# TensorE in written order with whole score units and projections three steps behind, and the second batch's first scores in the softmax gap

## The chip, the cores and the metric

One core of one Trainium2 chip runs the kernel. The metric is the device time in microseconds (us) of one execution, as a median of several. A difference under about 0.2% (4.6 us here) can't be told from no change.

## What is computed

There are four batches. In each, the columns of q and k (6080 tokens by 256 channels) are scaled to length one, a 256 by 256 matrix of scores between channels is formed over all tokens, a softmax is taken over its rows, and v is multiplied by it. The result, 24320 tokens by 256, goes through a two-layer network with a gated unit of 2048 columns.

```python
qn = q / (np.linalg.norm(q, axis=1, keepdims=True) + 1e-06)
kn = k / (np.linalg.norm(k, axis=1, keepdims=True) + 1e-06)
s = kn.transpose(0, 2, 1) @ qn / tau
a = np.exp(s - s.max(-1, keepdims=True))
a /= a.sum(-1, keepdims=True) + 1e-09
x = (v @ a).reshape(B * S, D)
h = x @ w_in
g = h * (1.0 / (1.0 + np.exp(-1.702 * h)))
out = g @ w_out
```

## The kernel before, in words

The attention of a batch ends in a 256 by 256 matrix, so the kernel folds it into the first layer: `weights` (L366) multiplies that matrix by w_in, and v goes straight through the product. Nearly all matrix work is done on numbers split in two parts, "hi" and "lo" (`split`, L77: ScalarE rounds to the hi part in a cast, VectorE subtracts to get the lo part), with three products hi·hi, hi·lo and lo·hi.

**The main loop** runs over four batches, 12 chunks of 512 tokens (the last has 448) and 16 slices `f` of 128 hidden columns: 768 steps. A step calls `hidden` (L396: six matmuls of 512 columns into a `ps_h` bank; then ScalarE's sigmoid L413, VectorE's product L414, ScalarE's cast to `gh` and VectorE's subtraction to `gl`) and, two steps behind (`DEPTH = 2`), `project` (L422: six matmuls into two `ps_o` banks that add up over the 16 slices). There are three `ps_h` banks, three `ps_o` banks and two banks `s0`, `s1` for the scores. In the first 32 steps the first two chunks take turns, so that each slice of w_in is used twice.

**The lead-in** (a `manual_schedule` block, so all engines in the written order) does the attention of batch 0 alone: `load` brings 128-partition pieces of q and k, `prepare` squares them (ScalarE) and adds the squares up (VectorE for batch 0), and `score` multiplies them as plain float32 (`direct`, L245: two records of 256 columns for each matmul, two output halves for each of the 48 token rows). Then come the norms (`norms_a`, L269: matmuls with a column of ones, `ps_n`; GpSimd takes a root; `norms_b` makes a diagonal matrix; `norms_c` spreads it by a matmul, `ps_b`), `softmax_a` and `softmax_c` on VectorE and ScalarE, four transposes (`ps_t`) and the first `weights` (`ps_w`, L372). While the softmax runs, `keep_warm` (L447) gives TensorE 18 and then 4 matmuls of ones.

**Side work of the main loop**: a dictionary from the step to functions that run after that step's `project`. In batch 0 it has the conversion of w_in and w_out from 64-bit words (`to_float32`, L102 to L132, steps 0 to 26), `win_split` and `weights` for the next three groups of slices; in batches 0 to 2 also the next batch's attention: `prepare` of a unit (two token rows of 128) and, three steps later, its `score`. There each row and half has one matmul of 512 columns (L250, hi part of k against hi and lo of q) and one of 256 (L258, lo part of k). Its squares are added up on GpSimd (L229). Batch 1's first unit is prepared at step 34. The order on each engine in the loop isn't the written one: a scheduler picks it from the dependencies and its own estimates when the program is built, and after that it is fixed.

Of the kernel before, what the change touches and what calls it, by code (L numbers as in the profile page):

```python
# [27 lines left out]
def channel_attention_then_glu(  # L28
# [137 lines left out]
    class Attention:  # L166
        def __init__(self, b, direct=False):
            self.b = b

            self.direct = direct  # L170
            self.raw = {}

            self.loads = [(0, UT)] + [(t, RT) for t in range(UT, T + 1, RT)]
            self.wh = [None] * NG
            self.wl = [None] * NG

            self.units = [(t, min(UT, T - t), P) for t in range(0, T, UT)]
            if TAIL:
                self.units.append((T, 1, TAIL))

        def load(self, t0, room):
# [4 lines left out]
            cuts = range(nt + 1) if self.direct and t0 == 0 else (0, nt)  # L186
            tiles = {}
            for a, z in zip(cuts, cuts[1:]):
                for src, tag in ((q, "raw_q"), (k, "raw_k")):
                    if tag not in tiles:  # L190
                        if self.direct:
# [14 lines left out]
        def prepare(self, u):  # L206
# [3 lines left out]
            rq, rk = (t[:pp, :nt, :] for t in self.raw[t0])  # L210
            if self.direct:
# [7 lines left out]
            for r, nm in ((rq, "acc_q"), (rk, "acc_k")):  # L219
# [4 lines left out]
                else:  # L224
# [3 lines left out]
                    eng = nc.vector if self.direct else nc.gpsimd  # L228
                    eng.tensor_tensor(acc, acc, sq, op=ALU.add)  # L229
            return qs, ks  # L230

        def score(self, u, qs, ks):
            t0, nt, pp = self.units[u]
            if u == 0:
# [4 lines left out]
            for j in range(nt):  # L239
                first = u == 0 and j == 0  # L240
                last = u == len(self.units) - 1 and j == nt - 1
                for i in range(NC2):
                    ci = slice(i * P, (i + 1) * P)
                    if self.direct:
                        nc.tensor.matmul(  # L245
                            self.s[i][:, :C], lhsT=ks[:, j, ci], rhs=qs[:, j, :],
                            start=first, stop=last,
                        )
                        continue
                    nc.tensor.matmul(  # L250
                        self.s[i],
                        lhsT=ks[:pp, j, 0, ci],
                        rhs=qs[:pp, j, :, :],
                        start=first,
                        stop=False,
                        skip_group_check=True,
                    )
                    nc.tensor.matmul(  # L258
                        self.s[i][:, C:],
                        lhsT=ks[:pp, j, 1, ci],  # L260
                        rhs=qs[:pp, j, 0, :],
                        start=False,
                        stop=last,
                        skip_group_check=True,
                    )

        def norms_a(self):
# [3 lines left out]
            for n in range(2 * NC2):  # L271
                acc, i = (self.acc_q, self.acc_k)[n // NC2], n % NC2
                if i == 0:
                    eng = nc.vector if self.direct else nc.gpsimd
# [31 lines left out]
        def softmax_a(self):  # L306
            self.x = small.tile([P, NC2, C], F32, tag="x", name="x")
            self.z = small.tile([P, NC2], F32, tag="z", name="z")
            m = small.tile([P, NC2], F32, tag="m", name="m")
            for i in range(NC2):  # L310
                x, z, mi = self.x[:, i, :], self.z[:, i : i + 1], m[:, i : i + 1]
                s = self.s[i][:, :C]
                if not self.direct:
                    nc.scalar.copy(x, self.s[i][:, C:])
# [74 lines left out]
    def v_split(b, c):  # L389
        w = chunks[c][1]  # L390
        raw = vtiles[b, c]
        vh = vp.tile([P, NC2, NCH], F32R, tag="v_h", name="v_h")
        vl = vp.tile([P, NC2, NCH], F32R, tag="v_l", name="v_l")
        split(vh[:, :, :w], vl[:, :, :w], raw[:, :, :w])
        vtiles[b, c] = (vh, vl)

    def hidden(at, b, c, f):
        w = chunks[c][1]
        vh, vl = vtiles[b, c]
# [15 lines left out]
        gh = gp.tile([P, NCH], F32R, tag="gh", name="gh")  # L415
        gl = gp.tile([P, NCH], F32R, tag="gl", name="gl")
# [37 lines left out]
    at = Attention(0, direct=True)  # L454
    nu = len(at.units)
# [4 lines left out]
    with tc.manual_schedule():  # L460
# [18 lines left out]
        win_fetch(3)  # L479
        wout_fetch(1)  # L480
        for u in range(nu - AHEAD, nu - 3):
# [149 lines left out]
```

## Time and profile before

| what | value |
|---|---|
| median of 3 runs (lowest, highest) | 2298.05 us (2297.94, 2298.36) |
| the profiled execution's own time | 2298.09 us |
| its span from first to last instruction | 2296.3 us |
| TensorE (PE), busy share of the span | 100% |
| VectorE (DVE), ScalarE (ACT), GpSimd (POOL) | 60%, 53%, 9% |
| granted TensorE clock | 1.0 |
| DMA queues, share of 16 engines' span | 14.0% |

The profile is of one execution. A row of a group gives line, engine, operation, output<-inputs, shape and count, then the busy time, the mean of one in ns, and the idle time before with what ended it. A timeline row gives start, duration, engine, line and how many instructions are merged; in brackets is the idle time before it with what released it. Matmuls overlap, so that the time one costs is the distance to the next start, not its duration. A matmul in plain float32 has two records, one in split form has one.

### The profile page before, as it was taken

The page shows a single profiled execution, that of the slowest core. Times are in us where ns is not written, and L with a number is a line of the kernel's source. Part 1 is how long each engine was busy: PE and PEld are TensorE (multiplying, and loading weights), DVE is VectorE, ACT ScalarE, POOL GpSimd, SP SyncE. Part 2 cuts the span into 40 slices and gives each one's busy share as a digit, 9 for nine tenths or more (in the row PEclk, how much of TensorE's full clock was granted, in tenths as well). Part 3 has the DMA queues.
Part 4 walks back from the last instruction along what each step waited for, and adds up shares of the span by engine and source line. Part 5 has one row for each costly group of instructions (what it writes and reads, how often), then busy time and mean ns, then how long its engine had stood idle before and what let it go on. Part 6 is the DMA issues. An engine that isn't in the chain of part 4 may idle for free.

```text
span 2296.3 us, 27390 instructions
## 1 busy us (share of the span) xinstructions
PE 2286.2 (100%) x10300; PEld 1906.7 (83%) x10300; DVE 1374.9 (60%) x2033; ACT 1224.0 (53%) x2108; POOL 212.3 (9%) x160
## 2 busy tenths in 40 slices
PE   9999999999999999999999999999999999999999
PEld 8878888888888888888888888888888888888888
DVE  7986666565565556565556556656555555555554
ACT  6765555555555555555455555554544444444444
POOL 0022322010020022010002012100000000000000
PEclk9999999999999999999999999999999999999999
DMA  8222111100111121110011111110000000000000
GB/s 309 92 74 74 56 55 61 57 27 19 37 54 56 37 74 56 35 56 18 19 56 46 46 56 56 55 35 28 18 19 28 27 19 28 28 19 28 27 9 18
DMA packets 46389, 109.77 MB, mean 48 GB/s; under 512 B 4528, under 2 KB 8624, under 8 KB 46256
## 3 DMA queue, kind: packets, MB, share of 16 engines
q1 hardware_dynamic: 46256, 108.02, 14.0%
q8 instruction: 80, 1.31, 0.2%
q14 instruction: 53, 0.43, 0.1%
HBM read 83.10 MB, written 24.90 MB: 47 GB/s over the span
## 4 chain that ended last, share of the span: by engine, by line
PE 96%; issue 2%; DVE 1%; ACT 0%; POOL 0%; POOLq 0%; DVEq 0%; ACTq 0%
PE ps_o L432 45%; PE ps_h L407 45%; PE s L250 3%; PE ps_w L372 2%; PE s L258 2%; DVE gl L79 0%; PE ps_x L451 0%; DVE z L127 0%; DVE g L414 0%; PE ps_n L276 0%; PE ps_b L299 0%; POOL rn L284 0%; DVE wl L79 0%; PE ps_t L344 0%; DVE z L121 0%
## 5 line engine op out<-in xcount | busy, mean ns | idle before, releaser
L414 DVE TENSOR_TENSOR g<-ps_h,g 128x512 f32<-128x512 f32 (+1 forms) x768 | 524.0, 683 | 456.9 <-ACT g L413 453.6
L79 DVE TENSOR_TENSOR gl<-g,gh 128x512 fp32r<-128x512 f32 (+1 forms) x768 | 566.1, 739 | 383.2 <-ACT gh L78 379.1
L413 ACT ACTIVATE g<-ps_h 128x512 f32<-128x512 f32 (+1 forms) x768 | 453.6, 592 | 508.4 <-PE ps_h L407 504.4
L78 ACT CAST gh<-g 128x512 fp32r<-128x512 f32 (+1 forms) x768 | 472.0, 615 | 442.7 <-DVE g L414 326.7
L407 PE MATMUL ps_h<-v_h,wh 128*128 128x512 f32 (+1 forms) x1536 | 598.0, 389 | 0.3 <-DVE g L414 0.3
L407 PE MATMUL ps_h<-v_h,wl 128*128 128x512 f32 (+1 forms) x1536 | 596.0, 388 | 1.6 <-DVE wl L79 1.6
L432 PE MATMUL ps_o<-gl,wo_h 128*128 128x512 f32 (+1 forms) x1536 | 596.0, 388 | 1.2 <-DVE gl L79 1.2
L407 PE MATMUL ps_h<-v_l,wh 128*128 128x512 f32 (+1 forms) x1536 | 596.3, 388 | 0.0
L432 PE MATMUL ps_o<-gh,wo_l 128*128 128x512 f32 (+1 forms) x1536 | 595.8, 388 | 0.0
L432 PE MATMUL ps_o<-gh,wo_h 128*128 128x512 f32 (+1 forms) x1536 | 504.2, 389 | 0.0
L407 PEld LDWEIGHTS ps_h<-v_h,wl 128*128 128x128 f32 x1536 | 288.6, 188 | 60.2 <-DVE wl L79 2.5
L407 PEld LDWEIGHTS ps_h<-v_h,wh 128*128 128x128 f32 x1536 | 288.7, 188 | 59.0 <-DVE g L414 1.3
L432 PEld LDWEIGHTS ps_o<-gl,wo_h 128*128 128x128 f32 x1536 | 288.6, 188 | 59.0 <-DVE gl L79 2.4
L432 PEld LDWEIGHTS ps_o<-gh,wo_l 128*128 128x128 f32 x1536 | 288.6, 188 | 57.1
L407 PEld LDWEIGHTS ps_h<-v_l,wh 128*128 128x128 f32 x1536 | 288.7, 188 | 54.2
L432 PEld LDWEIGHTS ps_o<-gh,wo_h 128*128 128x128 f32 x1536 | 286.6, 188 | 56.2 <-ACT win_h L78 0.2
L229 POOL TENSOR_TENSOR acc_q<-acc_q,sq 128x512 f32<-128x512 f32 (+1 forms) x72 | 93.8, 1303 | 1235.2 <-ACT sq L227 1082.8
L229 POOL TENSOR_TENSOR acc_k<-acc_k,sq 128x512 f32<-128x512 f32 (+1 forms) x72 | 112.2, 1558 | 11.1 <-ACT sq L227 10.8
L250 PE MATMUL s<-qs,ks 128*128 128x512 f32 (+1 forms) x288 | 109.1, 395 | 0.0
L258 PE MATMUL s<-qs,ks 128*128 128x256 f32 (+1 forms) x288 | 81.0, 281 | 0.0
L227 ACT ACTIVATE sq<-raw_q 128x512 f32<-128x512 f32 (+1 forms) x96 | 58.2, 606 | 34.0 <-DMA raw_q<-in_q 31.4
L79 DVE TENSOR_TENSOR v_l<-v_raw,v_h 128x1024 fp32r<-128x1024 f32 (+1 forms) x48 | 59.4, 1237 | 11.1 <-ACT v_h L78 10.0
(82 smaller groups left out, 928.0 us busy)
## 6 DMA issues: line engine op xcount, KB each, us to landing
raw_q<-in_q SPq DMA_DIRECT2D x44, 512.0 KB, 4.0
raw_k<-in_k SPq DMA_DIRECT2D x44, 512.0 KB, 4.4
v_raw<-in_vT SPq DMA_DIRECT2D x44, 512.0 KB, 3.8
out_T<-osb SPq DMA_DIRECT2D x88, 256.0 KB, 2.1
words<-in_w_in SPq DMA_DIRECT2D x8, 512.0 KB, 7.5
words<-in_w_out SPq DMA_DIRECT2D x8, 512.0 KB, 3.5
v_raw<-in_vT SPq DMA_DIRECT2D x4, 448.0 KB, 3.6
out_T<-osb SPq DMA_DIRECT2D x8, 224.0 KB, 2.0
```

The costliest lines, as they stand in the source:

```text
L78: ins = nc.scalar.copy(dst_hi, src)
L79: nc.vector.tensor_tensor(dst_lo, src, dst_hi.bitcast(F32), op=ALU.subtract)
L227: nc.scalar.activation(sq, r, AF.Square)
L229: eng.tensor_tensor(acc, acc, sq, op=ALU.add)
L250: nc.tensor.matmul(self.s[i], lhsT=ks[:pp, j, 0, ci], rhs=qs[:pp, j, :, :], start=first, stop=False, skip_group_check=True,)
L258: nc.tensor.matmul(self.s[i][:, C:], lhsT=ks[:pp, j, 1, ci], rhs=qs[:pp, j, 0, :], start=False, stop=last, skip_group_check=True,)
L372: nc.tensor.matmul(ps, lhsT=l[:, j, ci], rhs=r[:, j, :], start=n == 0, stop=n == 3 * NC2 - 1,)
L407: nc.tensor.matmul(ps[:, :w], lhsT=l[:, j, fs], rhs=r[:, j, :w], start=n == 0, stop=n == 3 * NC2 - 1,)
L413: newest[0] = nc.scalar.activation(g, ps[:, :w], AF.Sigmoid, scale=1.702)
L414: nc.vector.tensor_tensor(g, ps[:, :w], g, op=ALU.mult)
L432: nc.tensor.matmul(out[d][:, :w], lhsT=l[:, f, ds], rhs=r[:, :w], start=f == 0 and n == 0, stop=f == NF - 1 and n == 2,)
```

## The change

- TensorE runs the whole loop in the written order (`manual_schedule(engines={PE})`); the other engines are still scheduled. From step 26 (`WIDE`) on, `project` runs three steps behind instead of two, and `gh` and `gl` get two more buffers each in a pool that the conversions no longer use.
- `score` of a split unit issues all its 512-column matmuls and then all its 256-column ones.
- The first four units of batch 1 (`nxt = Attention(1, 4)`) are scored in plain float32 in the lead-in (`score_first`, 16 matmuls in groups of 3, 11, 1 and 1) in place of the 22 matmuls of `keep_warm`; their four loads are issued in the lead-in and stay in buffers of the `wh` and `wl` tags. Their squares are taken at steps 26, 28, 30 and 32, each behind the newest sigmoid on ScalarE (`pinned`). The other 21 units follow from step 35, also pinned in batch 0.
- In the lead-in, batch 0's unit nu-3 is scored ahead of the norms, and units nu-2 and nu-1 ahead of `norms_c`. The second load of batch 0 comes in two halves.
- Splits of v are cut in two halves, and later loads are issued four steps before their `prepare`.

```diff
-            self.loads = [(0, UT)] + [(t, RT) for t in range(UT, T + 1, RT)]
+            short = UT if self.alone else 0
+            self.loads = [(t, RT) for t in range(short, T + 1, RT)]
+            if short:
+                self.loads.insert(0, (0, short))
...
-            cuts = range(nt + 1) if self.direct and t0 == 0 else (0, nt)
+            cuts = (0, nt)
+            if self.alone and t0 <= UT:
+                cuts = range(0, nt + 1, 1 + t0 // UT)
...
+        def score_first(self, n):
+            ps = ps_o.tile([P, NCH], F32, tag="o", name="s_first")
+            todo = [(u, j, i) for u in range(self.direct) for j in range(UT) for i in range(NC2)]
+            for m, (u, j, i) in enumerate(todo):
+                rq, rk = self.fetched(u)
+                nc.tensor.matmul(
+                    ps[:, i * C : (i + 1) * C],
+                    lhsT=rk[:, j, i * P : (i + 1) * P],
+                    rhs=rq[:, j, :],
+                    start=m == 0, stop=m == len(todo) - 1,
+                    skip_group_check=True,
+                )
+                if m + 1 in n:
+                    yield
+            yield
+            self.x = small.tile([P, NC2, C], F32, tag="x", name="x")
+            nc.scalar.copy(self.x, ps.rearrange("p (c x) -> p c x", c=NC2))
...
+            for j, i in steps:
+                nc.tensor.matmul(
+                    self.s[i],
+                    lhsT=ks[:pp, j, 0, i * P : (i + 1) * P],
+                    rhs=qs[:pp, j, :, :],
...
+            for j, i in steps:
+                nc.tensor.matmul(
+                    self.s[i][:, C:],
+                    lhsT=ks[:pp, j, 1, i * P : (i + 1) * P],
+                    rhs=qs[:pp, j, 0, :],
...
-        for u in range(nu - AHEAD, nu - 3):
+        for u in range(0, nxt.direct, RT // UT):
+            nxt.fetched(u)
+        wout_fetch(1)
+        for u in range(nu - AHEAD, nu - 2):
             at.score(u, *ready[u])
         at.norms_a()
...
-        for u in range(nu - 3, nu - 1):
+        for u in range(nu - 2, nu):
             at.score(u, *ready[u])
+        s1 = nxt.score_first((3, 14, 15))
+        next(s1)
         at.norms_c()
-        at.score(nu - 1, *ready[nu - 1])
-        keep_warm(ones, 18)
+        next(s1)
         at.softmax_a()
         at.softmax_c()
         at.transposes(lambda: next(o0))
-        keep_warm(ones, 4)
+        next(s1)
...
+    with tc.manual_schedule(engines={mybir.EngineType.PE}):
...
+                for u in range(nu):
+                    if u < nd:
+                        put(WIDE + 2 * u, pinned, prep, u)
+                        continue
+                    at_u = first + 4 * (u - nd)
+                    put(at_u - 4, nxt.fetched, u)
+                    put(at_u, *((pinned, prep) if b == 0 else (prep,)), u)
+                    put(at_u + 3, score, u)
...
-                if len(late) > DEPTH:
+                if len(late) > (3 if wide[0] else 2):
                     project(*late.pop(0))
```

The order of instructions changes as follows. TensorE's order in the softmax gap, before: `s` are batch 0's scores, `ps_x` the matmuls of `keep_warm`, `ps_b` those of `norms_c`, `ps_t` the transposes, `ps_w` the weights.

```order
L276 MATMUL ps_n<-ones,acc_k 128x1 x2
L245 MATMUL s_167<-raw_q,raw_k 128x256
L245 MATMUL s_168<-raw_q,raw_k 128x256
L245 MATMUL s_167<-raw_q,raw_k 128x256
L245 MATMUL s_168<-raw_q,raw_k 128x256
L245 MATMUL s_167<-raw_q,raw_k 128x256
L245 MATMUL s_168<-raw_q,raw_k 128x256
L299 MATMUL ps_b<-diag,ones 128x128 x2
L245 MATMUL s_167<-raw_q,raw_k 128x256
L245 MATMUL s_168<-raw_q,raw_k 128x256
L451 MATMUL ps_x<-ones 128x128 x18
L344 MATMUL ps_t<-ident,x 128x128 x4
```

The same place after the change, where `s_first` are batch 1's first scores:

```order
L312 MATMUL ps_n<-ones,acc_k 128x1 x2
L275 MATMUL s_169<-raw_q,raw_k 128x256
L275 MATMUL s_170<-raw_q,raw_k 128x256
L275 MATMUL s_169<-raw_q,raw_k 128x256
L275 MATMUL s_170<-raw_q,raw_k 128x256
L250 MATMUL s_first<-raw_q,raw_k 128x256 x3
L335 MATMUL ps_b<-diag,ones 128x128 x2
L250 MATMUL s_first<-raw_q,raw_k 128x256 x11
L385 MATMUL ps_t<-ident,x 128x128 x4
L250 MATMUL s_first<-raw_q,raw_k 128x256
```

Between `ps_n` and `ps_b` stand four scores of batch 0 in place of six, none are left behind `ps_b`, and four more therefore stand ahead of `ps_n`; `s_first` fills the places of `ps_x`.

TensorE's order at one score unit of batch 1 before, with the numbers of the buffers (`gh_1510` is the `gh` of one step, whose `project` is cut in two here):

```order
L250 MATMUL s0_1560<-qs_1490,ks_1491 128x512
...
L432 MATMUL ps_o_1479<-gh_1510,wo_h_100 128x512
L258 MATMUL s0_1560<-qs_1490,ks_1491 128x256
...
L250 MATMUL s1_1561<-qs_1490,ks_1491 128x512
L258 MATMUL s1_1561<-qs_1490,ks_1491 128x256
L250 MATMUL s0_1560<-qs_1490,ks_1491 128x512
L258 MATMUL s0_1560<-qs_1490,ks_1491 128x256
L250 MATMUL s1_1561<-qs_1490,ks_1491 128x512
L258 MATMUL s1_1561<-qs_1490,ks_1491 128x256
```

A unit after the change:

```order
L285 MATMUL s0_1607<-qs_1535,ks_1536 128x512
L285 MATMUL s1_1608<-qs_1535,ks_1536 128x512
L285 MATMUL s0_1607<-qs_1535,ks_1536 128x512
L285 MATMUL s1_1608<-qs_1535,ks_1536 128x512
L294 MATMUL s0_1607<-qs_1535,ks_1536 128x256
L294 MATMUL s1_1608<-qs_1535,ks_1536 128x256
L294 MATMUL s0_1607<-qs_1535,ks_1536 128x256
L294 MATMUL s1_1608<-qs_1535,ks_1536 128x256
```

The eight matmuls of a unit stand together, with three pairs of neighbours of 256 columns, where the two widths took turns before, with projections of three steps between the first two.

ScalarE's order before, at the end of the conversions (`sq` are the squares that GpSimd adds up, `z` on L118 begins a conversion, here the last two):

```order
L227 ACTIVATE sq_1603<-raw_k_1592 128x512
L227 ACTIVATE sq_1704<-raw_q_1590 128x512
L227 ACTIVATE sq_1707<-raw_k_1592 128x512
...
L118 ACTIVATE z_1142<-words_1067 128x512
...
L227 ACTIVATE sq_1808<-raw_q_1798 128x512
L413 ACTIVATE g_1191<-ps_h_1184 128x512
L118 ACTIVATE z_1207<-words_1117 128x512
```

After the change, from the last conversion to the second unit's squares (`acc` is written by the first unit's squares alone, without an addition):

```order
L118 ACTIVATE z_1214<-words_1124 128x512
...
L462 ACTIVATE g_1300<-ps_h_1293 128x512
L234 ACTIVATE acc_q_1307<-raw_q_431 128x512
L234 ACTIVATE acc_k_1309<-raw_k_433 128x512
...
L462 ACTIVATE g_1338<-ps_h_1331 128x512
L238 ACTIVATE sq_1355<-raw_q_431 128x512
L238 ACTIVATE sq_1358<-raw_k_433 128x512
```

The squares of batch 1, and with them GpSimd's additions, stood among the conversions and stand behind the last of them now.

More of the change, by code (lines that the diff above doesn't have):

```diff
@@ L238, in score @@
                 ]
[L239 to L256, printed above, removed]
-                    )
[L258 to L265, printed above, removed]
+            steps = [(j, i) for j in range(nt) for i in range(NC2)]
@@ new lines, in score @@
+            last = u == len(self.units) - 1
+            if u < self.direct:
+                for j, i in steps:
+                    nc.tensor.matmul(
+                        self.s[i][:, :C],
+                        lhsT=ks[:, j, i * P : (i + 1) * P],
+                        rhs=qs[:, j, :],
+                        start=u == start and j == 0,
+                        stop=last and j == nt - 1,
+                    )
+                return
+            for j, i in steps:
[3 more added lines that the diff above has]
+                    rhs=qs[:pp, j, :, :],
+                    start=u == start and j == 0,
+                    stop=False,
+                    skip_group_check=True,
+                )
@@ L267, in norms_a @@
+            for j, i in steps:
+                nc.tensor.matmul(
+                    self.s[i][:, C:],
+                    lhsT=ks[:pp, j, 1, i * P : (i + 1) * P],
+                    rhs=qs[:pp, j, 0, :],
+                    start=False,
+                    stop=last and j == nt - 1,
+                    skip_group_check=True,
+                )
         def norms_a(self):
@@ L306, in softmax_a @@
         def softmax_a(self):
-            self.x = small.tile([P, NC2, C], F32, tag="x", name="x")
+            begun = not self.alone and self.direct
+            if not begun:
+                self.x = small.tile([P, NC2, C], F32, tag="x", name="x")
             self.z = small.tile([P, NC2], F32, tag="z", name="z")
@@ L387, in v_load, with v_split @@
         vtiles[b, c] = raw
-    def v_split(b, c):
+    vsplit = {}
+    def v_split(b, c, j=None):
         w = chunks[c][1]
         raw = vtiles[b, c]
[L392 to L395, printed above, removed]
+        if not j:
+            vh = vp.tile([P, NC2, NCH], F32R, tag="v_h", name="v_h")
+            vl = vp.tile([P, NC2, NCH], F32R, tag="v_l", name="v_l")
+            vsplit[b, c] = (vh, vl)
+        vh, vl = vsplit[b, c]
+        js = slice(None) if j is None else slice(j, j + 1)
+        split(vh[:, js, :w], vl[:, js, :w], raw[:, js, :w])
+    wide = [0]
     def hidden(at, b, c, f):
         w = chunks[c][1]
-        vh, vl = vtiles[b, c]
+        vh, vl = vsplit[b, c]
         grp, o = divmod(f, FG)
```

153 lines of the change are left out of this document (87 added, 66 removed).

## The prediction

> **What bounds the kernel now.** I read the page first: the busy times, then the chain that ended last.
>
> ```profile
> span 2296.3 us, 27390 instructions
> PE 2286.2 (100%) x10300; PEld 1906.7 (83%) x10300; DVE 1374.9 (60%) x2033; ACT 1224.0 (53%) x2108; POOL 212.3 (9%) x160
> PE 96%; issue 2%; DVE 1%; ACT 0%; POOL 0%; POOLq 0%; DVEq 0%; ACTq 0%
> ```
>
> TensorE is busy throughout and carries 96% of the chain. So a change helps only if it takes matmuls off TensorE or closes a gap in it. How full is it really? The chain gives the distance between matmuls in a quiet stretch, and the timeline of PE that of a score unit:
>
> ```profile
> 1884.57 2.27 PE ps_o L432 x10
> ```
>
> ```profile
> 174.14 0.39 PE L250 MATMUL s<-qs,ks 128*128 128x512 f32 x1
> 174.37 0.28 PE L258 MATMUL s<-qs,ks 128*128 128x256 f32 x1
> 174.48 0.39 PE L250 MATMUL s<-qs,ks 128*128 128x512 f32 x1
> 174.71 0.28 PE L258 MATMUL s<-qs,ks 128*128 128x256 f32 x1
> ```
>
> A 512-column matmul costs 0.227 us, a 256-column one 0.11 (174.37 to 174.48; I use half of 0.227, 0.113). The windows show where TensorE isn't full:
>
> ```profile
> 60.00:122.00 62.00, 61.45 (x269) 50.16 (x268) 57.00 (x100) 48.04 (x86) 4.90 (x2) 1.00 0.30 95
> 122.00:138.00 16.00, 13.37 (x57) 10.22 (x56) 16.00 (x20) 9.88 (x19) 9.94 (x7) 1.00 0.23 85
> 138.00:200.00 62.00, 62.00 (x278) 50.82 (x277) 38.63 (x57) 34.52 (x58) 5.96 (x4) 1.00 0.16 52
> ```
>
> Columns: width, then busy time and count of PE, PEld, DVE, ACT, POOL. In 122 to 138 us, 57 matmuls at 0.227 fill 12.9 of 16 us, and DVE is busy for all 16 with only 20 instructions. Later there is nothing to close. The rest to win is in the lead-in, in that stretch, and in the number of matmuls.
>
> **Scores taken out of the loop.** Four units, two rows, two halves: 16 matmuls of each width leave batch 1's loop, 16 x (0.227 + 0.113) = 5.4 us. Their place is full of TensorE work on both sides, so all of it counts: -5.4. ScalarE's casts and VectorE's subtractions of those units go too; both engines have slack (62% DVE in the third window).
>
> **The gap that takes them.** TensorE in the lead-in:
>
> ```profile
> 9.20 36.50 PE L245 MATMUL s<-raw_q,raw_k 128*128 128x256 f32 x168 [1.68 <-DMA raw_k<-in_k]
> 45.63 0.61 PE L276 MATMUL ps_n<-ones,acc_q 128*128 128x1 f32 x4
> ...
> 49.69 0.71 PE L299 MATMUL ps_b<-diag,ones 128*128 128x128 f32 x4 [0.31 <-DVE diag L292]
> 50.33 1.13 PE L245 MATMUL s<-raw_q,raw_k 64*128 64x256 f32 x4
> 51.38 4.29 PE L451 MATMUL ps_x<-ones 128*128 128x128 f32 x36
> 55.51 0.60 PE L344 MATMUL ps_t<-ident,x 128*128 128x128 f32 x4
> ...
> 56.78 0.73 PE L372 MATMUL ps_w<-win_h,aT_h 128*128 128x512 f32 x2
> ...
> 60.57 0.50 PE L407 MATMUL ps_h<-v_h,wl 128*128 128x512 f32 x1 [0.25 <-DVE wl L79]
> ...
> 64.79 0.51 PE L407 MATMUL ps_h<-v_h,wh 128*128 128x512 f32 x1 [0.30 <-DVE g L414]
> ```
>
> A plain float32 matmul has two records of 36.4 / 168 = 0.217 us, so 0.43 us. From 49.69 to 55.51 the chain is norms and softmax, not TensorE. The 16 first scores take 6.9 us; groups of 11, 1 and 1 fit where `ps_x` ran and where TensorE waits at 60.57. What moves against it: four scores of unit nu-3 go ahead of `ps_n`. TensorE arrives there at 45.63 without a wait, so they cost 4 x 0.43 = 1.7 us. Does the wait run behind `ps_n` absorb that? No: from `ps_n` to `ps_b` it is VectorE, GpSimd's root and VectorE again,
>
> ```profile
> 46.72 0.16 DVE L283 COPY rn<-ps_n 128x4 f32<-128x4 f32 x1 [0.81 <-PE ps_n L276]
> 49.87 1.22 DVE L79 TENSOR_TENSOR v_l<-v_raw,v_h 128x1024 fp32r<-128x1024 f32 x1
> 51.01 0.42 DVE L304 COPY rq<-ps_b 128x256 f32<-128x256 f32 x1
> 51.54 0.48 DVE L317 SCALAR_TENSOR_TENSOR x<-s,rn,rq 128x256 f32<-128x256 f32 x1
> 62.13 0.69 DVE L79 TENSOR_TENSOR wo_l<-z,wo_h 128x512 fp32r<-128x512 f32 x1
> ```
>
> and the softmax starts (51.54) behind `rq`, not behind the last scores. The whole chain shifts. Could TensorE reach `ps_n` earlier? The halved second load lets it start before 9.20, but then it needs the third load. SP issues a load when the eighth one before it has landed:
>
> ```profile
> 9.08 0.33 SPq L199 DMA_DIRECT2D raw_k<-in_k  x1
> ...
> 12.43 0.33 SPq L102 DMA_DIRECT2D words<-in_w_in  x1
> ...
> 17.60 0.33 SPq L199 DMA_DIRECT2D raw_k<-in_k  x1
> 18.88 0.33 SPq L199 DMA_DIRECT2D raw_q<-in_q  x1
> ...
> 51.12 0.38 SPq L386 DMA_DIRECT2D v_raw<-in_vT  x1
> ```
>
> ```profile
> 56.62 1.05 ACT L78 CAST v_h<-v_raw 128x1024 fp32r<-128x1024 f32 x1
> ```
>
> The issue at 9.08 is the landing of the second load's k (PE goes on at 9.20), that at 12.43 of the third load's k. Before, TensorE wanted it at 9.20 + 16 x 0.217 = 12.67. So it gains 0.2 us at most and waits at 11 to 12.4 instead. I take +1.6; the ends are -0.1 (all 1.7 regained and the wait at 9.20 gone) and +1.9 (smaller packets land later). Four loads of 512 KB stand ahead of others on SP's queue now, 1.3 us each (17.60 to 18.88). The v of the second chunk, issued at 51.12 behind them, isn't cast before 56.62, and later still with the shift, so I count nothing; uncovered it would be up to 5.1.
>
> **The loop's start.** In the old order six hidden units stand ahead of the first `gl` matmul. In the new one three do, done 18 x 0.227 = 4.1 us after a start near 61.7: 65.9. VectorE has wo_l, one conversion step, g, another two, g and then `gl`: from 62.13 + 1.6 = 63.7 some 5.5 instructions of 0.6 us (0.69 less the overlap with the next) and `gl`'s own 0.7, so 67.8. TensorE wants it at 66.1 and waits 1.6; its waits inside the first unit I put at 0.6, while the old ones (0.42 before 60.57, 0.46 before 64.79) were 0.9. Net +1.2. Further on, two steps of slack are 5.4 us against a chain of ScalarE and VectorE of four instructions of 0.6 to 0.7; with DVE at 92% in the first window this may fail now and then: 0 to +3.
>
> **Squares behind the conversions.** What fills VectorE in 122 to 138?
>
> ```profile
> 113.76 0.68 DVE L79 TENSOR_TENSOR gl<-g,gh 128x512 fp32r<-128x512 f32 x1
> ...
> 123.03 1.77 DVE L79 TENSOR_TENSOR gl<-g,gh 128x512 fp32r<-128x512 f32 x1
> ```
>
> ```profile
> 122.78 1.48 POOL L229 TENSOR_TENSOR acc_q<-acc_q,sq 128x512 f32<-128x512 f32 x1
> 124.22 1.74 POOL L229 TENSOR_TENSOR acc_k<-acc_k,sq 128x512 f32<-128x512 f32 x1
> ```
>
> ```profile
> 132.44 0.50 PE L432 MATMUL ps_o<-gl,wo_h 128*128 128x512 f32 x1 [1.25 <-DVE gl L79]
> ...
> 136.62 0.50 PE L407 MATMUL ps_h<-v_h,wl 128*128 128x512 f32 x1 [1.39 <-DVE wl L79]
> ```
>
> The same `gl` takes 0.68 us alone and 1.77 beside GpSimd's addition of batch 1's squares. TensorE then waits for `gl` and for `wl`. The new order has no square before the last conversion, and no split of batch 1 either. So the 3.1 us of the second window (16 less 12.9) go, ends -3.1 and 0. Afterwards the squares meet a VectorE at 62%, where the third window has such additions and no idle TensorE.
>
> **Units in one piece.** At the 64-row tail the old order goes in and out of 64 rows:
>
> ```profile
> 458.37 0.39 PE L407 MATMUL ps_h<-v_h,wl 128*128 128x512 f32 x1
> ...
> 460.77 0.40 PE L432 MATMUL ps_o<-gh,wo_l 128*128 128x512 f32 x1
> ```
>
> Six matmuls of 512 and two of 256 lie between these starts, 1.6 us of 2.4. One visit costs about 0.4 (in the lead-in 50.33 to 51.38 is 1.05 for four records of 0.217, with as much again shared on the way in and out), so -0.4 in each of three batches, -1.2. The other effect is that 256-column matmuls now follow one another, so that the next weights load under 0.113 us. The load's own row says 0.188:
>
> ```profile
> L258 PEld LDWEIGHTS s<-qs,ks 128*128 128x128 f32 x282 | 53.0, 188 | 8.1
> ```
>
> But already now a 512-column matmul starts 0.11 after a 256-column one (174.37 to 174.48), its weights loaded in that time. I take 0, ends 0 and 201 x (0.188 - 0.114) = +15 (three pairs in each of 65 units and one in each of six short ones). The Trainium skill, TensorE: Matmul & The Clock Gate, LDWEIGHTS (loading the stationary operand), gives a load as its columns over 1.2 GHz: 107 ns by estimate, which would just fit, where the PEld row would not; the 0.11 speaks for the page.
>
> **The rest** lies off TensorE: halves of v, more `gh` buffers, the third step of delay (8.2 us of slack for 5.4), earlier loads. Its cover is a TensorE that is busy 62.00 of 62.00; without it each would be some 0.1 us a step.
>
> **Sum** against the profiled execution's 2298.09 (span 2296.3 and 1.8 around it; the median, 2298.05, is the same): -5.4 + 1.6 + 1.2 - 3.1 - 1.2 = -6.9, 2291.2.
>
> **Rivals.**
> - *The lead-in isn't later.* If the early loads land sooner than SP's rows make them, TensorE meets `ps_n` at 45.6 and the +1.6 falls away: 2289.6. For it: the hole of 1.68 us at 9.20 is about the same size. Against it: 12.43. Chance 0.2.
> - *The collision moves.* GpSimd's additions at steps 26 to 32 slow `gl` there, or the strict order loses in the conversions what the pinning gains: 2291.2 + 3.1 = 2294.3. For it: DVE 16 of 16. Against it: the third window. Chance 0.17.
> - *The scores aren't free in the gap*, because their loads or the norms leave TensorE late by as much as the loop saves: 2291.2 + 5.4 = 2296.6, no real change. Against it: 5.8 us between `ps_b` and `ps_t`. Chance 0.08.
> - *Weights show between narrow matmuls*, in the 71 units of batches 1 to 3: +15, 2306, slower. It decides from 34 ns a pair (6.9 us over 201), and is slower beyond doubt from 57 ns. For it the PEld row, against it 174.48. Chance 0.1.
> - My forecast has 0.45.
>
> **Numbers.** Forecast, first and second rival hold 0.82. Low: 2289.6 less the loop's 1.2 is 2288.4, say 2288.2. High: 2294.3 and 1.8 more at the loop's start, 2296.1. Faster than 2293.5 (0.2%) are the forecast, the first rival and a little of the second, less the forecast's own upper end: 0.65. Slower: the last, 0.1. Between: 0.25.
>
> **What would show it.** Right: `ps_n` starts near 47.2, the softmax near 53.1, the first `ps_o` waits for `gl` near 66 to 68; no PE wait near 130 to 140 and no POOL addition before the last `wo_l`; 256-column matmuls 0.11 apart; 272 matmuls of each width. Wrong: `ps_n` still at 45.6 (first rival); pairs of 256 columns 0.15 or more apart (last rival); a run of PE waits for `gl` or for the splits of q and k in the loop, which would say that the written order is worse than the scheduled one.

## The result, and the profile after

| | median us (lowest to highest, runs) | ratio to before, 95% interval |
|---|---|---|
| before | 2298.37 (2297.94 to 2299.69, 6) | |
| after | 2287.05 (2285.47 to 2288.67, 6) | 0.9949 [0.9937, 0.9961] |
| after, measured again later | 2288.82 (2285.26 to 2289.90, 5) | 0.9954 [0.9941, 0.9968] |

The change takes 9.6 to 11.3 us off; the prediction said 6.9. The second measurement was expected within 1 us of 2287 and came out 1.8 above it. The profiled execution of after took 2288.67 us (1.8 of it outside the span) and is the slowest of its six. The page:

```profile
span 2286.9 us, 27146 instructions
PE 2277.1 (100%) x10256; PEld 1901.9 (83%) x10256; DVE 1379.7 (60%) x2073; ACT 1240.4 (54%) x2145; POOL 219.2 (10%) x160
PE 98%; DVE 1%; DMA 1%; ACT 0%; SPq 0%; issue 0%; ACTq 0%
```

TensorE has 44 records fewer: 32 left the loop, 44 went with the 22 matmuls of ones, and 32 came with the 16 plain ones. It is still nearly the whole of the chain. The waits of PE:

```profile
PE s L275 <- DMA raw_k<-in_k: 3.5, 3, 2.4
PE ps_o L484 <- DVE gl L79: 1.4, 3, 0.9
```

Columns: total, times, longest. The waits at 132.44 and 136.62 are gone; 3.5 us of waits stand ahead of the lead-in's scores, where before had 1.7. The timeline of PE there:

```profile
4.34 1.89 PE L275 MATMUL s<-raw_q,raw_k 128*128 128x256 f32 x8
7.12 1.96 PE L275 MATMUL s<-raw_q,raw_k 128*128 128x256 f32 x8 [0.89 <-DMA raw_k<-in_k]
9.32 1.97 PE L275 MATMUL s<-raw_q,raw_k 128*128 128x256 f32 x8 [0.24 <-DMA raw_k<-in_k]
13.65 36.46 PE L275 MATMUL s<-raw_q,raw_k 128*128 128x256 f32 x160 [2.36 <-DMA raw_k<-in_k]
49.94 0.50 PE L312 MATMUL ps_n<-ones,acc_q 128*128 128x1 f32 x4
...
63.94 0.58 PE L456 MATMUL ps_h<-v_h,wh 128*128 128x512 f32 x1
...
70.21 0.50 PE L484 MATMUL ps_o<-gl,wo_h 128*128 128x512 f32 x1 [0.93 <-DVE gl L79]
```

`ps_n` is at 49.94 and the first hidden matmul at 63.94. In the trace of before the latter stands at 59.69, so the lead-in is 4.25 us longer here. The rest, from the first hidden matmul to the end of the span, I call **the loop**: 2296.3 - 59.69 = 2236.6 us before, 2286.9 - 63.94 = 2223.0 after, that is -13.6.

**Where the loop's 13.6 us went.** I took the distance of every PE start past 70 us to the next one, and subtracted what the columns cost in a quiet stretch (0.4427 ns each, 226.7 for 512). What is left is 24.0 us before and 15.4 after. Distances over 30 ns too long ("stalls") hold 10.8 and 6.8 of it, the other 512-column matmuls 9.2 and 4.2, the rest (448 columns and fewer) 4.0 and 4.4. So 8.6 us less are lost, and the scores taken out are the other 5.4 (up to 70 us the loop loses 0.8 more than before, and behind the last matmul's start it is 0.4 shorter, which closes the sum). The 5.0 us behind 512-column matmuls that are no stalls had no term in the prediction. The chain around 300 us shows them. Before (start, us, what):

```profile
301.67 1.36 PE ps_h L407 x6
...
305.75 0.23 PE s L250
305.98 0.12 PE s L258
306.09 0.69 PE ps_h L407 x3
306.78 0.47 PE ps_o L432 x2
307.25 0.23 PE ps_h L407
307.48 0.91 PE ps_o L432 x4
```

After:

```profile
299.82 0.91 PE s L285 x4
300.73 0.47 PE s L294 x4
301.20 1.39 PE ps_h L456 x6
302.59 1.36 PE ps_o L484 x6
303.95 1.36 PE ps_h L456 x6
```

Six undisturbed matmuls take 1.36 us (0.227 each). Behind a 256-column one (L258, L294) the next six take 1.39: in before three take 0.69 and the next two 0.47 instead of 0.68 and 0.45. In before some 280 narrow matmuls stand alone, so this happens up to 280 times; in after they come in 68 groups, nearly all of four.

### The profile page after: what moved, and what is told of

The parts are those of the page before. It is cut to its first block, busy times and chain, and to the rows that moved or that the text cites. A ratio compares the mean times of both kernels' runs of the same rounds, so it can differ in the third digit from the quotient of the medians.

```text
span 2286.9 us, 27146 instructions
## 1 busy us (share of the span) xinstructions
PE 2277.1 (100%) x10256; PEld 1901.9 (83%) x10256; DVE 1379.7 (60%) x2073; ACT 1240.4 (54%) x2145; POOL 219.2 (10%) x160
## 3 DMA queue, kind: packets, MB, share of 16 engines
q1 hardware_dynamic: 45680, 108.02, 14.1%
## 4 chain that ended last, share of the span: by engine, by line
PE 98%; DVE 1%; DMA 1%; ACT 0%; SPq 0%; issue 0%; ACTq 0%
PE ps_o L484 45%; PE ps_h L456 45%; PE s L285 3%; PE ps_w L413 2%; PE s L275 2%; PE s L294 1%; DMA raw_k<-in_k 0%; PE s_first L250 0%; DMA raw_q<-in_q 0%; DVE v_l L79 0%; SPq L206 0%; PE ps_n L312 0%; DVE gl L79 0%; DVE g L463 0%; ACT sq L238 0%
## 5 line engine op out<-in xcount | busy, mean ns | idle before, releaser
L79 DVE TENSOR_TENSOR gl<-g,gh 128x512 fp32r<-128x512 f32 (+1 forms) x768 | 548.2, 715 | 463.7 <-ACT gh L78 462.2
L484 PE MATMUL ps_o<-gh,wo_h 128*128 128x512 f32 (+1 forms) x1536 | 594.8, 387 | 0.0
L79 DVE TENSOR_TENSOR v_l<-v_raw,v_h 128x512 fp32r<-128x512 f32 (+2 forms) x94 | 76.0, 847 | 4.6 <-ACT v_h L78 4.6
L285 PE MATMUL s<-qs,ks 128*128 128x512 f32 (+1 forms) x272 | 73.5, 390 | 0.0
L238 ACT ACTIVATE sq<-raw_k 128x512 f32<-128x512 f32 (+1 forms) x96 | 58.1, 605 | 7.5 <-DMA raw_k<-in_k 3.3
```

Of the source, the lines that this page charges most:

```text
L79: nc.vector.tensor_tensor(dst_lo, src, dst_hi.bitcast(F32), op=ALU.subtract)
L238: nc.scalar.activation(sq, r, AF.Square)
L285: nc.tensor.matmul(self.s[i], lhsT=ks[:pp, j, 0, i * P : (i + 1) * P], rhs=qs[:pp, j, :, :], start=u == start and j == 0, stop=False, skip ...
L484: nc.tensor.matmul(out[d][:, :w], lhsT=l[:, f, ds], rhs=r[:, :w], start=f == 0 and n == 0, stop=f == NF - 1 and n == 2,)
```

## The experiments

Four theories were put against each other. A: a matmul of 256 columns slows the 512-column ones behind it, so that fewer and longer groups of them make the loop shorter. B: TensorE's written order, with the third step, is what steadies the loop. C: the halved second load makes the third load's k late, and TensorE stands and then runs at half clock. D: the halves help or do nothing, and the unit moved ahead of the norms alone makes the lead-in late. Fourteen kernels ran, and the changed one a second time. Columns: median and ratio to before; from the profiled execution, the start of `ps_n` and of the first hidden matmul, the loop, the stalls in it, and what the other 512-column distances lose.

| run | median us | ratio, 95% | ps_n | hidden | loop | stalls | wide |
|---|---|---|---|---|---|---|---|
| before | 2298.37 | 1 | 45.6 | 59.7 | 2236.6 | 10.8 | 9.2 |
| after | 2287.05 | 0.9949 [0.9937, 0.9961] | 49.9 | 63.9 | 2223.0 | 6.8 | 4.2 |
| after, again | 2288.82 | 0.9954 [0.9941, 0.9968] | 51.7 | 65.7 | 2222.4 | 7.8 | 4.1 |
| e1 widths in turn | 2290.07 | 0.9963 [0.9950, 0.9975] | 47.7 | 61.7 | 2223.8 | 6.2 | 6.1 |
| e2 narrow alone | 2292.90 | 0.9977 [0.9967, 0.9986] | 49.5 | 63.5 | 2228.8 | 8.4 | 9.6 |
| e3 second load whole | 2285.76 | 0.9949 [0.9936, 0.9961] | 49.1 | 63.1 | 2223.7 | 7.5 | 4.2 |
| e4 and unit after norms | 2285.80 | 0.9948 [0.9935, 0.9962] | 45.3 | 61.0 | 2222.7 | 6.4 | 4.2 |
| e5 no first scores | 2292.68 | 0.9975 [0.9965, 0.9984] | 50.5 | 64.3 | 2227.8 | 5.9 | 4.3 |
| e6 squares unpinned | 2307.92 | 1.0040 [1.0025, 1.0055] | 48.5 | 69.6 | 2236.0 | 21.5 | 4.3 |
| e7 TensorE scheduled | 2284.29 | 0.9940 [0.9927, 0.9952] | 47.4 | 61.4 | 2221.1 | 5.7 | 4.2 |
| e8 two behind | 2308.41 | 1.0045 [1.0030, 1.0060] | 50.4 | 64.4 | 2245.8 | 29.4 | 4.4 |
| e9 narrow made wide | 2315.61 | 1.0075 [1.0060, 1.0090] | 47.8 | 61.8 | 2251.3 | 7.2 | 2.4 |
| e10 eight in a row | 2284.03 | 0.9938 [0.9925, 0.9950] | 45.3 | 59.7 | 2222.2 | 6.5 | 3.1 |
| e11 before, pinned | 2294.39 | 0.9985 [0.9976, 0.9993] | 47.2 | 61.2 | 2232.9 | 6.7 | 9.5 |
| e12 scheduled, two behind | 2288.47 | 0.9960 [0.9948, 0.9973] | 46.8 | 60.8 | 2225.4 | 9.1 | 5.4 |
| e13 together | 2283.01 | 0.9935 [0.9923, 0.9948] | 45.2 | 60.5 | 2220.5 | 5.7 | 3.8 |
| e14 before, halves | 2298.82 | 1.0005 [0.9996, 1.0014] | 48.5 | 62.4 | 2236.5 | 10.8 | 9.2 |

The lead-in differs by microseconds between executions with the same code (after and after again, e1, e2, e7, e8, e9), so a loop edit is judged by its loop first. Four executions have the same loop code (after, after again, e3, e4): their loops lie between 2222.4 and 2223.7 us and their wide losses between 4.1 and 4.2, so that a difference under about 1.4 us in the loop isn't clear of chance. Each ratio is to before as it ran beside that kernel, with medians from 2297.78 to 2298.40.

### What makes 512-column matmuls slow: e1, e2, e9

e1 issues the widths in turn inside a unit, as before did:

```diff
-            for j, i in steps:
                 nc.tensor.matmul(
                     self.s[i][:, C:],
```

> The changed kernel with one edit: a score unit stays in one piece and in the written order, but its 512- and 256-column matmuls take turns as they did before. Theory A (narrow matmuls slow those that follow; 280 lone ones cost about 30 ns each before, 68 groups cost 46 ns each after): from the old trace's eight in a row, 174.14 to 175.43, some 45 ns inside and 27 behind a unit against 46 now, so the loop (first hidden matmul to the end, 2223.0 us in the changed kernel, 2236.6 before) gets 1.5 to 4 us longer. Rival B (the written order of hidden units and projections, or the third step of delay, is what steadied the matmuls): no change, within 0.5 us.

The loop got 0.9 us longer, less than theory A's 1.5 to 4 and more than rival B's 0.5, and not clear of chance: the wide loss grew by 1.9, which is, while stalls and narrower matmuls lost 1.1 less. The median is 3 us over after's first six and 1.3 over its second five; three of e1's five runs had a mean clock below 1.0, so the median says little of the loop. A narrow matmul with one 512-column matmul behind it slows just that one, by 8.7 ns in the mean over 269; the effect is there and small.

e2 keeps the unit's wide matmuls together and spreads its four narrow ones over the next steps, so that each stands alone:

```diff
-            for j, i in steps:
+            def narrow(j, i):
                 nc.tensor.matmul(
...
+            for j, i in steps:
+                self.narrow.append((narrow, j, i))
+            self.one_narrow()
...
+                    for later in (4, 5, 6):
+                        put(at_u + later, nxt.one_narrow)
```

> The changed kernel with one edit: the four 512-column matmuls of a score unit stay together, but of its four 256-column ones only the first follows them, and the others come one in each of the next three steps, each between a projection and a hidden unit. Theory A: 272 lone narrow matmuls at about 30 ns are 8.2 us where 68 groups are 3.1, so the loop is about 5 us longer (2228), and the mean distance of 512-column matmuls goes back from 227.1 towards 227.6 ns. Rival B (the written order steadied them): no change, within 0.5 us.

The loop is 5.8 us longer, 5.4 of it in the wide distances, which lose what they lose in before (9.6 and 9.2). The chain of e2, where a stretch of 1.39 follows every single narrow matmul:

```profile
303.95 0.11 PE s L295
304.06 1.39 PE ps_h L466 x6
305.45 1.36 PE ps_o L494 x6
306.81 0.12 PE s L295
306.92 1.39 PE ps_h L466 x6
```

Position by position, over 266 narrow matmuls, the next five distances are 5.8, 9.1, 1.7, 5.8 and 4.2 ns too long, together 27, and the sixth and later ones 0.

e9 leaves everything in place and gives the narrow matmuls 512 columns. It adds the product of the two low halves, which the kernel leaves out:

```diff
-                    self.s[i][:, C:],
+                    self.s[i],
                     lhsT=ks[:pp, j, 1, i * P : (i + 1) * P],
-                    rhs=qs[:pp, j, 0, :],
+                    rhs=qs[:pp, j, :, :],
```

> The changed kernel with each 256-column matmul of a score unit made 512 columns wide (it also adds the product of the two low halves, which the kernel leaves out), in the same place and from the same tiles. Some 272 matmuls grow by 0.113 us, 30.8 us. Theory A (what slows the followers is the narrow width itself): the excess behind and inside the 68 groups, 46 ns each or 3.1 us, goes: 2287.05 + 30.8 - 3.1 = 2314.7, and the mean of the 512-column distances that are no stalls falls to about 226.9 ns. Rival (it is the visit to the scores' tiles that slows, whatever the width): the followers stay slow by 27 ns a group: 2317 or more, and the mean stays at 227.1.

2315.6 lies between the 2314.7 of theory A and the 2317 or more of the rival. The mean 512-column distance decides: it is 226.93 ns (226.9 expected by theory A, 227.1 by the rival, 227.15 in after). The chain of e9:

```profile
302.45 0.91 PE s L285 x4
303.36 0.91 PE s L294 x4
304.26 1.36 PE ps_h L456 x6
305.62 1.36 PE ps_o L484 x6
```

Same tiles, same place, no 1.39. The narrow width itself, with the half-wide input and output that go with it, is what slows the followers. What in TensorE does it was not tried.

### The lead-in: e3, e4, e14

e3 takes the halves of the second load back; e4 also scores unit nu-3 behind the norms again:

```diff
-            if self.alone and t0 <= UT:
-                cuts = range(0, nt + 1, 1 + t0 // UT)
+            if self.alone and t0 == 0:
+                cuts = range(nt + 1)
...
-        for u in range(nu - AHEAD, nu - 2):
+        for u in range(nu - AHEAD, nu - 3):
...
-        for u in range(nu - 2, nu):
+        for u in range(nu - 3, nu):
```

> The changed kernel with the second load of batch 0 in one piece again. Theory C (the halves brought the third load in 1.1 us later, 13.5 for 12.4, and left TensorE idle for 2.4 us in one piece, so that its clock fell to half for 3.4 us, which costs 1.7): the third load's k is in by 12.4 to 12.6, no half clock, the norms' first matmul starts at 47.2 to 47.5 instead of 49.9, and the time falls by 2 to 3 us against the changed kernel and spreads less from run to run. Rival D (the halves help or do nothing, and the lead-in is late by the unit moved ahead of the norms alone): no change or slower.

> As the kernel with the second load whole, and also unit nu-3 of batch 0 scored behind the norms' first matmuls again, as before the change; the first scores of batch 1 stay in the gap. Theory C and the prediction's own +1.6 us for that unit: the norms start at 45.6, their spreading matmuls wait for six scores and three first scores (3.9 us for 3.1 of chain), so 0.8 of the 1.7 comes back as a late start there: 0.8 to 1.6 us faster than the kernel with the second load whole. If the unit's place doesn't matter: no change.

Both are 1.3 us under after's first median and 3.0 under its second, too little to be told apart, and e4 is level with e3, where 0.8 to 1.6 less was expected. The profiled execution of e3 doesn't bear theory C out: the third load's k, by the issue row behind it, is in at 13.61 and not by 12.6, `ps_n` is at 49.1 and not at 47.2 to 47.5, and the clock is halved after all, behind the wait for the second load. So it is in e11 (below), which has the lead-in of before. The timeline of PE in e3 and then in e11:

```profile
9.60 39.62 PE L275 MATMUL s<-raw_q,raw_k 128*128 128x256 f32 x176 [2.60 <-DMA raw_k<-in_k]
```

```profile
9.22 38.18 PE L245 MATMUL s<-raw_q,raw_k 128*128 128x256 f32 x168 [2.05 <-DMA raw_k<-in_k]
```

Ahead of `ps_n` the clock was halved in 6 of the 11 profiled executions with halves and in 2 of the 6 without, so the halves aren't needed for it. The issue row that marks the third load's k stands at 12.03 to 14.26 with halves (13.4 in the mean) and at 11.95 to 13.61 without (12.4). The halves go with a k that lands 1.0 us later in the mean, but the two ranges overlap.

e4 has `ps_n` back at 45.3, as before, but its first hidden matmul at 61.0: behind `ps_n` three units and three first scores now stand ahead of `ps_b`, which starts at 51.4 though its `diag` is done at 49.4. So with the three first scores there the unit costs about as much behind `ps_n` as ahead of it; e10 (below) takes them away.

e14 puts the halves alone into before:

```diff
-            cuts = range(nt + 1) if self.direct and t0 == 0 else (0, nt)
+            cuts = (0, nt)
+            if self.direct and t0 <= UT:
+                cuts = range(0, nt + 1, 1 + t0 // UT)
```

> The kernel before with one part of the change alone: the second load of q and k in halves. Prediction's reading: TensorE gains 0.2 us at most in the lead-in, the time stays within 0.5 us of before. Theory C: the third load's k lands about 1 us later, TensorE stands for 2 us or more ahead of it, ps_n starts 1 to 2.5 us later than 45.63, and more of the runs show the half clock behind that wait: 2299.5 to 2301.

The timeline of PE in e14:

```profile
9.70 1.96 PE L247 MATMUL s<-raw_q,raw_k 128*128 128x256 f32 x8 [0.62 <-DMA raw_k<-in_k]
13.89 34.73 PE L247 MATMUL s<-raw_q,raw_k 128*128 128x256 f32 x152 [2.23 <-DMA raw_k<-in_k]
48.46 0.50 PE L278 MATMUL ps_n<-ones,acc_q 128*128 128x1 f32 x4
```

`ps_n` comes 2.8 us later than before's, a little more than theory C's 1 to 2.5: 1.2 by the later load and 1.6 by the half clock behind the wait. The median moved by only 1.0 us, in between the two expectations, and the interval holds no change: the size differs from run to run, and only 3 of 11 runs had a mean clock of 0.999. Why the third load's k lands later with the second in halves (the issue behind it is at 13.77 here and 13.53 in after, 12.43 in before) stays open.

### The first scores: e5

```diff
-    nxt = Attention(1, 4)
+    nxt = Attention(1, 0)
...
-        next(s1)
+        keep_warm(ones, 18)
```

> The changed kernel (2287.05) with the second batch's first four units back in the loop, and 18 and 4 keep-warm products in the lead-in in place of their scores. If the first scores are free in the gap, as the prediction had it, the loop alone gets longer: 16 x (0.227 + 0.113) = 5.4 us, plus 0.2 for what four more groups of narrow matmuls slow behind them (46 ns each), and the lead-in stays within 0.5 us: 2292.6. If they are not free (the prediction's third rival), the first hidden matmul comes earlier by 2 us or more and the time stays below 2290.

2292.68 against 2292.6 (an agreement to 0.1 is luck, with after's own medians 1.8 apart); the loop is 4.9 us longer and the lead-in 0.3. From `ps_n` to the first hidden matmul it is 13.75 us here and 14.00 in after, so the 16 scores cost 0.25 us in the gap: they are as good as free.

### Pinning, the third step and the written order: e6, e8, e7, e11, e12

e6 lets batch 0's preparation of batch 1 run where the scheduler puts it; e11 pins it in before, and changes nothing else:

```diff
-                        put(WIDE + 2 * u, pinned, prep, u)
+                        put(WIDE + 2 * u, prep, u)
...
-                    put(at_u, *((pinned, prep) if b == 0 else (prep,)), u)
+                    put(at_u, prep, u)
```

```diff
-                put(first + 4 * u, prep, u)
+                put(first + 4 * u, *((pinned, prep) if b == 0 else (prep,)), u)
```

> The changed kernel with batch 0's preparation of batch 1 no longer pinned behind the conversions, so that its squares may run among them. If the collision of GpSimd's additions with VectorE was what made TensorE wait (the prediction's -3.1), waits for gl and wl come back between 110 and 140 us, 2.6 to 3.7 us in sum: about 2290. If the third step of delay alone covers it, TensorE waits less than 1 us there: 2287 to 2288.

> The kernel before with one part of the change alone: the preparation of batch 1 pinned behind batch 0's conversions. The trace of before loses 3.7 us between 128 and 140 us. If the collision costs that and the pinning alone takes it away, as the prediction had it: 2294.6 to 2295.2. If pinning only pays where TensorE's order is written (or moves the collision), 2297 or above.

e11 is right to 0.2 us: -4.0, and past 70 us no wait of PE over 0.1 us is left in its loop (two of 0.3 stand ahead, as in before). e6 is far beyond both numbers, +20.9. The waits of PE in e6 show where:

```profile
54.27 0.49 PE L335 MATMUL ps_b<-diag,ones 128*128 128x128 f32 x2 [1.29 <-DVE diag L328]
...
63.51 0.72 PE L385 MATMUL ps_t<-ident,x 128*128 128x128 f32 x4 [2.77 <-DVE x L376]
...
110.19 0.79 PE L484 MATMUL ps_o<-gl,wo_h 128*128 128x512 f32 x1 [3.14 <-DVE gl L79]
110.78 0.63 PE L484 MATMUL ps_o<-gh,wo_l 128*128 128x512 f32 x1
111.20 0.63 PE L484 MATMUL ps_o<-gh,wo_h 128*128 128x512 f32 x1
...
138.67 0.49 PE L484 MATMUL ps_o<-gh,wo_h 128*128 128x512 f32 x1 [1.05 <-ACT gh L78]
142.24 0.79 PE L484 MATMUL ps_o<-gl,wo_h 128*128 128x512 f32 x1 [3.07 <-DVE gl L79]
```

and the additions of GpSimd beside them:

```profile
59.49 1.28 POOL L240 TENSOR_TENSOR acc_k<-acc_k,sq 128x512 f32<-128x512 f32 x1 [4.14 <-ACT sq L238]
...
107.27 1.71 POOL L240 TENSOR_TENSOR acc_k<-acc_k,sq 128x512 f32<-128x512 f32 x1
...
138.23 1.72 POOL L240 TENSOR_TENSOR acc_q<-acc_q,sq 128x512 f32<-128x512 f32 x1
```

Four units' loads are in place early, so their squares run into the softmax too, and into the conversions in two places. A wait of 3.1 us in the written order is a stop of TensorE, and behind each of the two the clock is at half for 6.8 us, in which matmuls start 0.43 us apart (110.78 to 111.20) instead of 0.23. So the pinning isn't worth a fixed 3 us: it is worth 4 in before and about 20 in the changed kernel. The two differ in the written order and in the four units that are there early; which of these makes it 20 was not separated.

e8 runs two steps behind throughout, e7 leaves TensorE's order to the scheduler, e12 does both:

```diff
-                if len(late) > (3 if wide[0] else 2):
+                if len(late) > 2:
```

```diff
-    with tc.manual_schedule(engines={mybir.EngineType.PE}):
+    if True:
```

> The changed kernel with projections two steps behind all along. If the third step does nothing for TensorE (the prediction counted it at nothing), the loop stays within 0.7 us: 2286.5 to 2288. If it steadies a strict order (theory B), TensorE waits for gl in many more places than the two or three of the changed kernel, and the loop grows by more than 2 us: 2289 or above.

> The changed kernel with TensorE's order in the loop left to the scheduler again; squares pinned, third step and widths apart stay (80 groups of narrow matmuls where there were 69). If the written order brings only the 64-row tails (the prediction's -1.2) and the groups, the loop grows by 1.2 + 11 x 0.046 = 1.7 us at most: 2287 to 2289. If the written order as such is what makes the change gain (theory B), the loop grows by 4 us or more: 2291 or above.

> The changed kernel with TensorE's order left to the scheduler and projections two steps behind: both edits, of which the first alone took 2.5 to 4.5 us off and the second alone cost 21. If the third step only pays for the written order (the scheduler puts other matmuls where a projection would wait), TensorE doesn't wait for gl and only what is slow behind more groups of narrow matmuls comes on top (131 groups instead of 80, 1.4 us at 27 ns each): 2285 to 2287. If the third step is needed whatever the order: 2295 or above.

The waits of PE in e8, for what a projection needs:

```profile
PE ps_o L484 <- DVE gl L79: 12.5, 16, 2.1
...
PE ps_o L484 <- ACT gh L78: 3.0, 5, 1.0
```

and in e12:

```profile
PE ps_h L456 <- DVE g L463: 0.7, 2, 0.4
...
PE ps_o L484 <- DVE gl L79: 0.2, 1, 0.2
```

e8 costs 21 us: 15.5 are these waits, and most of the rest follows them, two stretches of half clock among it. With the scheduler's order two steps lose 0.2 us to `gl`. e12 is 4.2 us over e7 where at most 2.7 was expected: 1.3 is in the wide distances (131 groups of narrow matmuls against 80), 3.4 in stalls: 1.2 at 64-row tails that are visited several times, 1.3 at the chunk ends near 650 and 1217 us and 0.7 at 441. e7 is the surprise: it is 2.8 us faster than after's first median, 4.5 than its second, where no gain was expected; its loop is 1.3 to 1.9 us shorter, below all four loops of after's code, and its lead-in has the code of after but caught its loads earlier. So theory B falls: the written order gains nothing. By the loops it costs 20 us with two steps (e8 against e12) and 1.3 to 1.9 with three (after against e7). The third step is worth 4.3 us of loop in the scheduler's order too (e12 against e7), and that is why after, with both, still has a loop 2.4 to 3.0 us shorter than e12, which has neither. Why the scheduler's order is 1 to 2 us better in the loop was not tried.

### The parts together: e10, e13

e10 starts from e4, issues the narrow matmuls of two units together, and moves the first scores from ahead of `ps_b` (11, 2, 1 and 2 instead of 3, 11, 1 and 1). e13 is e10 with the scheduler's order.

```diff
-        s1 = nxt.score_first((3, 14, 15))
-        next(s1)
+        s1 = nxt.score_first((11, 13, 14))
...
+            self.narrow.append((u, qs, ks))
+            if len(self.narrow) < 2 and not last:
+                return
```

> The kernel of the fourth experiment (2285.8), with the narrow matmuls of two units together, eight in a row, and with the first scores of the second batch taken from ahead of ps_b: 11 behind ps_b, 2 behind ps_t, 1 behind ps_w and 2 where TensorE waits for the first gl. Lead-in: ps_b comes when diag is there, 1.3 us earlier, and with it the softmax and the first hidden matmul, near 59.7 instead of 61.0. Loop: by theory A half of the 68 groups keep a slow stretch behind them, -34 x 0.027 = -0.9 us. In sum 2283.6. If eight narrow matmuls in a row show their weight loads (188 ns against 113), 136 x 0.075 = 10 us are lost: above 2292.

> The best of the parts together: second load whole, three units behind the norms, eight narrow matmuls in a row, first scores behind ps_b, and TensorE's order in the loop left to the scheduler. The lead-in of the eight in a row (first hidden matmul at 59.7) and the loop 1.5 us shorter than there, if the scheduler's gain in the loop is independent of the rest: 2284.0 - 1.5 = 2282.5. If it is not: 2284 or above.

The chain of e10:

```profile
307.84 0.91 PE s L286 x4
308.75 0.95 PE s L302 x8
309.70 1.39 PE ps_h L465 x6
```

Eight in a row take 0.119 each and show no weight loads; the wide loss falls by 1.1 (0.9 expected), the first hidden matmul is at 59.7, as before the change. So the lead-in needs hardly to get longer: from `ps_n` to the first hidden matmul it is 14.5 us, 14.1 in before and 15.8 in e4, where three first scores stand ahead of `ps_b`. Both kernels come out within 0.5 us of what was expected. e13, 2283.01, is the fastest of all: 0.65% under before, and below every run of after (2285.26 at the least).

## Why the prediction was right and wrong

The time fell by 9.6 to 11.3 us and not by 6.9; the first median is 1.2 us under the low end of 2288.2. Two steps failed, in opposite directions, so that a part of their errors cancels. The loop has -13.6 where the prediction's terms add up to -8.5, mostly by 4.6 us from a term that it put at nothing or worse. The lead-in has +4.25 in the profiled execution where it has +1.6.

- **Scores taken out, -5.4: right**, and free in the gap as said (e5: time to 0.1 us, loop 4.9 of 5.6). The third rival is out.
- **The lead-in, +1.6: right in its own term, wrong in what it left out.** The unit ahead of `ps_n` costs 1.7, and in e7, with after's lead-in, `ps_n` is at 47.43 (47.2 predicted). In after's own profile it is at 49.94, 4.3 late: 1.7 for the unit, 1.0 for the third load's k (TensorE goes on at 13.65, and 12.67 was wanted) and 1.7 for the clock, which is halved for 3.4 us behind that wait, so that eight records cost 0.21 us more each. The failed step is "it gains 0.2 us at most", with 0.3 at the upper end for later loads and nothing for the clock; the upper bound +1.9 was 2.4 us too low for that execution. That the halves alone make the load late isn't shown (e3), and the half clock comes without them too (e3, e11). The first rival falls: in all executions with after's lead-in `ps_n` is at 46.8 to 51.7.
- **The loop's start, +1.2: right in kind.** The first `gl` is waited for at 70.21 for 0.93 us (1.6 predicted near 66 to 68, and the lead-in is later by 2.6); net the start lost 0.8.
- **Squares behind the conversions, -3.1: right, a little small.** e11 alone gives -4.0: the stalls around those two waits were 3.7 in sum, as each wait has smaller losses behind it.
- **The 64-row tails, -1.2: right.** Stalls at the 64-row matmuls are 2.8 us before and 1.2 after, -1.6.
- **Units in one piece, 0 with ends 0 and +15: wrong in sign, and the main error.** The step that failed is to price a narrow matmul by its own distance alone. Its own distance is 0.11 to 0.12, as read, but it costs the five behind it 27 ns more. Fewer such places are -4.6 (the wide loss -5.0, the rest +0.4). The prediction had said "Later there is nothing to close", from a window with TensorE busy 62.00 of 62.00; a full busy share doesn't show distances that are 9.2 us too long in sum. No row in a page shows this; the chain's 0.69 for three and 0.47 for two did, in the trace of before. The last rival falls: four in a row take 0.47, eight 0.95. The Trainium skill, TensorE: Matmul & The Clock Gate, LDWEIGHTS (loading the stationary operand), has a weight load of 128 columns at 107 ns by estimate; 0.119 a matmul agrees, and the 0.188 of the PEld rows doesn't bind.
- **The rest, nothing: wrong reason, and 1.4 too little.** "8.2 us of slack for 5.4" took the chain of `gl` at its busy time. With two steps the written order has 21 waits for `gl` and `gh` (e8). The third step isn't worth nothing: it is worth 4.3 us of loop in the scheduler's order (e12 against e7), and the written order, which brings nothing itself, can't do without it. At two chunk ends and at 175 us the three steps don't cover it either, 1.4 us with what follows.
- **The collision moves** (second rival): not in after; the additions start at 149 us, behind the last conversion. It is what e6 does.

The sum of the loop by these: -5.4 - 4.1 (stalls, e11) - 1.6 - 4.6 + 1.4 + 0.4 (start +0.8, end -0.4) = -13.9, measured -13.6; the lead-in's +4.25 in that execution leaves -9.4 for the two spans.

## What to carry to other kernels

Where a matmul of half width stands between full ones, look at the distances behind it and not only at its own; put such matmuls side by side, which cost one slow stretch for four or eight. A written order on a saturated engine must have a slack for each wait that the scheduler would have filled, so test the order and its slack apart: here the order without the slack cost 21 us, and the slack without the order had a loop 1.3 to 1.9 us shorter than both together. A busy share of 100% doesn't mean that nothing is left to win; compare the distances with those of a quiet stretch. A wait that stops TensorE for 2 us can cost nearly as much again in clock (1.7 here).

## What the runs showed of the hardware

**Narrow matmuls.** A 256-column matmul in split form slows the next five of 512 columns by 27 ns in sum (e2), and nothing when it has 512 columns itself (e9).

**The clock.** The windows of after, with PEclk as the column behind POOL:

```profile
9.00:13.00 4.00, 2.04 (x9) 1.44 (x8) 1.57 (x4) 1.41 (x3) 0.00 (x0) 1.00 0.97 393
13.00:17.00 4.00, 3.35 (x9) 2.75 (x10) 3.34 (x6) 3.03 (x6) 0.00 (x0) 0.66 1.03 415
17.00:21.00 4.00, 4.00 (x18) 3.48 (x17) 2.75 (x5) 2.46 (x5) 0.00 (x0) 0.92 1.03 410
```

The clock was cut to half for 3.41 us, or twice that, and its changes lie on a grid of 3.413 us that goes through the whole execution. I counted, for every piece of that grid that ran at full clock, in all 17 traces from 3 us on, how much of it TensorE was busy, going by its starts and the cost of a record. In 13 pieces it was 35% or less, and the next piece ran at half clock each time; in all others it was 42% or more, and the next ran at full clock. So, in these executions, waits for loads of up to 1.85 us left the clock alone (before 1.68, e1 1.80, e6 1.85), and those from 1.96 us cut it (e2 1.96, e11 2.05, e14 2.23, after 2.36, e3 2.60). What counts is how much of one piece of the grid a wait takes. The Trainium skill, TensorE: Matmul & The Clock Gate, What's actually happening, gives a free-running window of 3413 ns, which agrees; its advice in Why this matters for your kernels, no gaps over about 3 us, is too generous here.
